# Twelve of 72 weight chunks get their low bits on VectorE alone, in a kernel whose order of work is written out as a string

## The chip, the cores and the metric

The kernel runs on one core of one Trainium2 chip. The metric is the device time of one execution in microseconds. Times before are the median of three runs; one further execution was profiled.

## The reference, cut to what matters

Attention within clusters (16 heads in two batches, 768 positions, head size 64) is followed by two blocks of dense layers over 1,536 tokens:

```python
mask = argmax(q_n . c_n) == argmax(k_n . c_n)        # per head, 16 centroids
attn = softmax(where(mask, q @ k.T / 8, -1e9))
x = attn @ v                                          # to [1536, 512]
h = x @ w_in
g = where(h >= 1, h, where(h <= -1, 0, (h + 1)**2 / 4))
x = g @ w_out                                         # 2048 -> 512
out = ((x @ w1) * (x @ w2)) @ w3 @ w_out2
```

The weights arrive as 64-bit floats and are used as 32-bit ones. The kernel makes each 32-bit pattern from the two 32-bit words of the 64-bit number. That is the work that the change is about.

## The kernel before, in words

**Tiling.** A head pair is a unit: four units for batch 0, four for batch 1. Each unit's attention is cut into 12 tiles of 128 queries by 768 keys, numbered 0 to 95 over the whole kernel; tiles 0 to 47 are batch 0. A tile goes through a score matmul on TensorE (`s`, L859, four instructions into one of four PSUM buffers), a row maximum on VectorE (`smax`, L867), a scale on GpSimd (L872), an exponential on ScalarE (`sexp`, L880), in batch 0 a transpose on TensorE (`spT`, L897) and a copy to SBUF on ScalarE or VectorE (`sT`, L352 or L354), which frees the PSUM buffer. Half a unit ends with a product with v (`pv`, L968) and a transpose of the reciprocal row sums (`ro`, L954). Queries and keys are each split into a rounded part (half-width casts of 64x768: `qh`, `kh`, `k2h`, `q1h`, `qh0`) and a remainder (low parts: `qlo`, `klo`, L357). The clusters come from projections onto the centroids (`am`, L539) and an argmax on VectorE (`ah`, L555 to L573).

**Weight chunks.** 72 chunks of 128x512 numbers are loaded as pairs of 32-bit words and turned into 32-bit floats by the function `chunk`. Each takes four operations: an absolute value with a scale of the high words on ScalarE (`wabs`, L1107), a floor of the low words on ScalarE (`wr`, `low_floor`, L1111), which leaves their top three bits as a number, a shift left by three and an OR on VectorE (`wc 2`, `shift_low`, L1115), and the sign by an AND and an OR on VectorE (`wc 3`, `sign`, L1121). 40 chunks are made in the attention of batch 0. Most of the first 24 are then split into a rounded part (`whi`, a chunk cast, L352 on ScalarE or L354 on VectorE) and a remainder (`wlo`, a chunk subtraction, L357 on GpSimd or VectorE), and multiplied into each other on TensorE (`wp`, L1169), with partial products copied out (`wpe0`) and added later (`wpe`, L1193). Others are stored to DRAM (`wd`, on SP's queue). Batch 0's dense layers run under batch 1's attention, and batch 1's layers after that (L1239, L1492).

**Start.** Eight loads of queries and keys and those of v go out on SP's queue, weight loads on ScalarE's. 40 filler products of the identity with itself (`idle`, L469) stand between TensorE's first steps; tile 6 may not start before all are done.

**Order.** Every step is declared with `add`: its name, the engines that may take it with a planner's costs, its needs and the buffers that it takes and frees. The planner's result is not computed in the kernel. It is written out in `ORDER`, a string of two letters for each of 3,036 steps: the pair, read as a number in base 88 and divided by two, gives the step, and the remainder which of its engines takes it. Each engine works its own steps in this order. Nothing else sets the order of the work.

```python
i, alt = divmod(LETTERS.index(a) * len(LETTERS) + LETTERS.index(b), 2)
```

Of the kernel before, what the change touches and what calls it, by code (L numbers as in the profile page):

```python
# [35 lines left out]

LETTERS = "#$%&()*+,-./0123456789:;<=>?@ABCDEFGHIJKLMNOPQRSTUVWXYZ[]^_`abcdefghijklmnopqrstuvwxyz|~"
ORDER = (
    "###%#*#,#0#.$.$V%X#(%V%[#2$0#4%e%h%c%q$6$8$:$<$>$X$_$a$c$e%b%k$2$4$H%]:m:|%y&,%_%i;0;>$@$B$D%m;L$]$Z$q#B$g$i"
# [4 lines left out]
    ",4,(,*,,,6<6<F<J&9<L<N<8<:<<&E&I<?+m+|,#,.&K,8,:,<<s,%<V,0,2,><g&>%%<@,@,L=*=:<e,B,D+g,N,P,F,R,X,Z,],_<i<k<Z"
    "<n<]<p,e,g<`<a;|<0<2,H,T,a,J<u+i+l,u,w=J<w=X<y<|+o=#%@&@&B<B<Q<R,V,c,y,|=,=<=i=>-(&P=.-#-*+r-,-.-4-6-%-8-:=0"
    "<q=%&c-0-2=@+s=2=4=6=B=D=(%>=y=N-<-@&U-B-D=L=Z=]-L,i,l=P=R=U=V&L-X-Z-]-N-P>0=_,m,o-F->=k>@=a=m=o=d=e=q=s>#-_"
    "=|>P-R-H-u-K-w-y>%>(>4>2>6-e-g=8=F,r-a.(.*.,>D-T-V&_-c&i>a-|>8,s=g=u>+&l&o&e&[=H>-.4.6.8=w>:&W&^&R&b&n>B>F>H"
    ".#-i-m>K&X>L&u..>o.%.0-k.@.B.3.D-o?#>.>=>>%*>e&s.L.N>R>T>V>c&g?4.:.X.<.Z>N>q>s-q.F>X>Z%B.P.R.T.>?(>g>u?%.]?F"
    "._>i.H.J.V>w?*>l>z>]?,?.?0>n>~.a.u.c?V/(/4/*/,&z&|/@-s.w/B/D(&?8?i?@&w>_?2?B?D/.(-($%,/6?6&q?J?H((%D.m.y.|/#"
    "?:?L(.?Z?X?]?<?N/8/:/<?>/%?_?k?m?o?a?Q?q?R/0/2/>%.%0%2.e.g?y%4?s?u/F%F/L/N%H%6/H%J?T?c?e@2@B/J/X%L%8@T@#/P/R"  # L50
    "/T@,?g%:%</Z.i.k?|@4@e0(0*@%.o@(@*/]/_/e/g/V.q?w@.@0/a/c.s@w@6/u/w(*@D0,0.@8@:@=/y@>%N040608@F@H@J@X/|/m@i@V"
    "@g@Z00%P0#0%%R@k@m@]@`@a@N@L@o%T@@@PA.0:020<0?0@0L0N0P0B0D@y@|/i/k/oA2A#A%A)A*0X@q@RA:@c@s@u0u0w0y0FA@0R0T/q"
    "0Z0]APAcA0A40H0J0W0|0_A,A<A>0e0gABADAF(0(2/sA6A8(4(61#0a0c1(1*0iAs1416ATARAVAX0lAZAH1,1.AeAgAiA]AkAKAM1%181:"
    "AwB%0m0o1012AmAo1X1Z1@1L1N1P1B1D1](:Au(=ANA_AaB,1<1R1T(8(AAy(>(BA|(MB#(N1_1FAqB(1H1>B*(D1e1g1J1V(FBJ(H1a1d0r"
    "1i2*(Z(J0s2,2.1u1k1w1y20B.B022(P1|(R24Bi1m1o1rC.BLBO1s2#2%26(TBkBmB2B4B6CL2((V(X282:2<B8B>B@Ck2>BBC12F2H2J2@"
    "2B2DBPBR2LBTBDB;2NB=BV2PBFBIB]B_BaBcBfC2C4C6FLC82T2V2XCNFe2c2eBXCQ2gC:Bg2RBZ2Z2^2_BoBqC<BsB|C#2i2kC?D0BuBxC&"
    "C(2m2a2oC@CBCD3%3(C+(]3*BzCRCTCn3,CoCWCFCH3436383/D>30D3C_CaCcCeC,CX3:3<D#3>2q323B2y3@CK(b3D(d(_(e3P3RCZD@D4"
    "D6D%DLD(3F3HD*3K3L3NCg(h3T3VDZ3XC^3ZD:CjD9CqCsCuCwDB2s3_D<3a3cDN3m3]D]3oCz(iDi3q3e3hDDDG3i3k(tD-E.3sG#(lDHDJ"
    "DPDR2u(nD_4>Da3u3wDk2w2|DTEL(pDn(uC~3#3y4042FP44463|Dc4@4B)(DVE1E2(w4D4GDeDg(q484:4H4JEkD/DYF0ENF>EP(yDoDqDs"
    "4L4N4<4PFiDuDxFND|E#4RFR4#EnFTEoE%E(4TGL4VDz4XFg4ZE4E6E*Fk4]4_E-FmFoE8E:4%4(E@EBF24aG(4*4,Gu4.FVF54c4e4gEEEF"  # L60
    "G%E<E?EI(|)#)%)*G*G,G.F#5:F%F(F*ERETEWEXEKHDE_5<5>F@F6F8FBEaE[E]GPEcEe5@Gy4i4k4m5B5D5FGNGRGT4oEqFYFZEsEuEwF:"
    "4q4s4uF-4w4y4|FqFsEyHmGwG|FHH#F<5H5JHHF/I,EhFJHFEjHJHLGVH%HNFDFFHq5#5,5.5LG05%5(FaFc5*G3E~F]FyF|HoHsHu5N5PHw"
    "F_FuGXGZH)IDI05V5X5R5T5ZH+I.FwI2I4I]G@GBGDGF5]5e5g5i5_5aGHGJ),G4G6).G9)1I65cIa)2G]G_5kHQGa5mHR)4G:G<5s50545u"
    "5oIH52Gc565wGfGgIF5qIJILIN58Iu5y5|6#GiGk6(6*G>GmJDI_HzHTIcGo)66,HV)9GrH~Gs6.60HXHZIe626%64):)<)>H86DH:H<H>H,"
    "H.H0I#6FH26H6R6TI%I8I:JmIyJHIwH@JFI|)AJ#J%)BJJ6JHaHc6V6XHeHgJLI(HCH5JNIgIPIi6Z6]6L6N6PH]6_H_I@K466IRI<I>JqKT"
    "Ik6a6cI*6eJo686g6i)D)FIB6o6q6sHiK86k6mJsJuK66uJ)K:6>IT6w6y6|J*H6IVIXIZJQJSK<K>)NImIoKuKXKVKZHl7#6:6<Jw)H)J)L"
    "K]KyJ,J.Kw6@6BK|L<7%J0J2JTJVJXJZL#7(7*7,IqJ5J6JzJ|Is7.70J^J_LTJ8J:J<J>727476K@KBL%)PK_J@JaJcJeL@JgJiJk7N7PJC"
    "K#K%K)7RKaKcK*KDKF78L>LB7TLV7:LuKH7<KJLD7>7V7XK,K.7@L)L*K0K2KLM4LHLXKeKgLwKNKP7]7_7a7c7eKRLZL]KiLyKm7k7m7gKk"
    "L|MTM#L,L.7oKo7q)T7BLaLcLJ7ZLF7sKr7u7i7wL_KsM8)RM6M%L0)V)X7y7|L47HMVL6L8L2MX8#8%8(Mm8.808284)Z8*L:M:M<LLLeM)"
    "M*MZN48<8>LP8@)_LNLg86Mo)cLS888,8:M]M_Lm7D7F7J7LM>LoM@Ma)^)a)e)gMCLiM,M.8X8Z8B8D8FM0NLN8LqMqMDLl8]8_8g8aMLN6"  # L70
    ")iMdMsLtMu8HNmN:MFMzM~N<M28i8k8mNPMHMeMJ8oMNMiMQMSO,NN)k)m8c8q8sNRN,NA8eNoNqMhNTNCNYNs8J8LNZ8R)o)qNVOLMw)sMk"
    "N.O0NuNw8u8w8y9*9,9.N#N%N)N*NyO.O2O4N~N>90928|OeNDNFOP9496NHNJO8O:Ne9#9%N0O69(NgP,8N8P8T8VONOROTOVN]N_NaOYN2"
    "989:9<9F9H9J9>O#O&O<NdO[9LP0OgP.9T9VNiNk9A9BPD9DO>OiOk9N9POmO(P2OrOsO*O@O]PeOo9R9c9e9gOCODP4OFP69q9sOaOdO_9i"
    "PF9k9mP8OuPHPJPLP;9XPQP#OwP%9u9w9y:%:(:*9|Q#PgOHPN9o:#9[PiOJP(P*PkPSQ%QDPmQ(Q*Q,Po9]9_9aQ.Oy:,:.P@PBP<:4:6Pr"
    "Q0:8:0P]PT:2QN:::=:>PsP>:B:D:F:HPuO|Q3Qa:JP_PbPV:P:RQG:@:TPwQI:L:N:VPX:XPyQ4Q6Q9QQQRP|QJQ<:ZQcQeQkR#PcP[Q;QL"
    "QTQVQ>QAQB:]:gRcR.R_Ra:_:a:cR@QmQp:e:iQZQ^QgR]:kR%R)QiRfS4RJQqQwR*S2RgRjRkR0S)R3S0S9S6QXQ_S]S@SCSEQsQuS;S_SU"
    "SWS=S?RCS$RnRESeSXRvRwSmQySLRqToR,RpRLShROSQR4R:RtTqRzS[R6R8SaSdSOR<R>Q|RFRHSrStS+SjS&SSSuSyS~R~SlTxT#S,T&Tz"
    "TsU%V(SHT~U*SxRPRRU.RTT(T6SGV*SKT,T:U-RVRYRZT0T<SoT.TvT>T@U0U#S.U2U4U6V,V.W:TPTRT2TBTZT]T*T8TFTTTWV0V2V4U(V6"
    "THT_TaTcW<TJU:UBUHU>ULTXV8T4TDUNV<V@VBU<UJW>W@V>TLTNU@UPURUXUZU]TeUcUeTgVEVHXLWBU8WDWFTiTkVLV:UDU_UTTmUmWJUo"
    "UaUgUiWOUqVZUsUkVGWIUuXNXZVTUFUVUwVPW_V_VaVJVRVcWRWmWMUyU|V#VeV%WPVNV]VVWcXPXRVuVwWVWXWZVyXiXwY,VkVnXUX^WaX`"  # L80
    "VgWoWqV|Y.XVXXW%W#X#W(VoXlXmVqVsW*W,XzXeXaX|Z>X&W.WUX(X*XcW^Y5XhY0Y6XoWgWsY9Y:X,Y3Y<YAVXXsViW0ZBZ@YBYDY?WeWu"
    "ZEWwYG[PXqYPY`YTYcZFYHYKWiWyW2W4W7W8ZcZrX8X.X1[_YLZNX:X2ZIX5XuX6Y(Y*ZSZTZKZL[mX<Y#WkW|XBZQYRZeX?X@Ya[S[TXDXF"
    "XIYoYqYs[b[c[oZsYXYeY&XJZgYVZVZX[VYN[(ZZZ_Z][q[ZZk[*[,[/YvYw[|]0[0]2YgYi^BYyY|Z#]#Z%[XYZ[e[iYk[]ZuZ(Z*Z-Y]Ym"
    "ZwZ.]&]8[k]:]<]?]@]D]H]FZ4ZaZ6Z8[w[s^D]4]6Z1Zi[g]C]M]QZyZ2Z|[u^FZ:Z<^J],[y](]K[2[4]N[6^H_T^L_c[8^gZm[#]TZo]X"
    "[:].]]]V]*_V_X[<^u[%]d[>[@[C^N^Q[D]Z^i_q_Z^R_e_h^V^[[F[H^_^a[J]g[L[N__]S]e_s_]`%]i]s_i^w_,^U]k]u]m_a`4]w^c]z"
    "_m]|`B_v_|^#_w^Y`)^%^(`6^+^,_._0`+_o_k_2`u_4`#`8^e^]a*a]`E`F^k^y^o_y^|a_^q_(_@_C]_]o^.^0^m_#_D_%_6]a]q_8^8^:"
    "^s`,^2^4_:`0_*^<_J_G^6ae_Hamagaqai_M_<auak^?_N_P^@aw`x`yaya|_R`H`J_>ap`:`<as`]bR`X`[```>a-a/`@`L`.aabT`N`e`P"
    "`aad`S`hcH`|a#`2`m`pa%a@`T`WaC`db[b]b_bVbYa(a4a6a9aHa0a2aDb(bwa:a=`ib#aGb*bya?`laKb.cLcJbcbgbbcOaTaWb0b&bjd>"
# [1669 lines left out]
```

## Time and profile before

| what | value |
|---|---|
| three runs, median | 719.14 us (718.37 to 720.06) |
| profiled execution, device time | 719.4 us |
| its span | 717.7 us |
| TensorE, VectorE, ScalarE, GpSimd busy | 697.5, 615.3, 467.4, 279.6 us |
| floors of low words on ScalarE (L1111) | 72, of 767 ns on average |
| shift with OR (L1115), sign (L1121) on VectorE | 72 each, of 695 and 726 ns on average |

The span runs from the first to the last instruction of the profiled execution; its device time is 1.7 us longer. Busy times of different engines overlap. The matmuls of TensorE are pipelined and their ends are modelled, so its busy time includes stretches in which it works below its peak; the busy time of its weight loads says how dense a stretch is.

### The profile page before, as it was taken

The page shows a single profiled execution, that of the slowest core. Times are in us where ns is not written, and L with a number is a line of the kernel's source. Part 1 is how long each engine was busy: PE and PEld are TensorE (multiplying, and loading weights), DVE is VectorE, ACT ScalarE, POOL GpSimd, SP SyncE. Part 2 cuts the span into 40 slices and gives each one's busy share as a digit, 9 for nine tenths or more (in the row PEclk, how much of TensorE's full clock was granted, in tenths as well). Part 3 has the DMA queues.
Part 4 walks back from the last instruction along what each step waited for, and adds up shares of the span by engine and source line. Part 5 has one row for each costly group of instructions (what it writes and reads, how often), then busy time and mean ns, then how long its engine had stood idle before and what let it go on. Part 6 is the DMA issues. An engine that isn't in the chain of part 4 may idle for free.

```text
span 717.7 us, 12011 instructions
## 1 busy us (share of the span) xinstructions
PE 697.5 (97%) x4185; PEld 633.1 (88%) x4185; DVE 615.3 (86%) x1087; ACT 467.4 (65%) x873; POOL 279.6 (39%) x351
## 2 busy tenths in 40 slices
...
GB/s 323 85 147 232 296 212 217 293 246 232 229 187 194 227 204 228 193 222 222 232 213 239 227 224 186 136 196 120 45 103 88 46 59 73 59 61 74 87 63 56
DMA packets 122509, 121.58 MB, mean 169 GB/s; under 512 B 80656, under 2 KB 89296, under 8 KB 122448
## 3 DMA queue, kind: packets, MB, share of 16 engines
...
## 4 chain that ended last, share of the span: by engine, by line
PE 80%; ACT 5%; DVE 5%; issue 2%; DMA 1%; ACTq 0%; POOL 0%; SPq 0%; DVEq 0%; POOLq 0%
PE mo L1239 37%; PE sc L1492 9%; PE sc L859 7%; PE mo L1492 6%; PE sc L1239 5%; PE av L976 3%; PE mo L1169 3%; PE av L1239 3%; PE sc L897 2%; PE av L968 2%; PE av L1492 2%; ACT P L880 2%; DVE nm L867 1%; ACT pt L352 1%; DMA wf<-wp 1%
## 5 line engine op out<-in xcount | busy, mean ns | idle before, releaser
L1239 PE MATMUL mo<-X,whl 128*128 128x384 f32 x912 | 169.0, 338 | 0.8 <-DVE Yp L354 0.8
L1239 PEld LDWEIGHTS mo<-X,whl 128*128 128x128 f32 x912 | 158.5, 188 | 3.1 <-DVE Yp L354 1.2
L357 POOL TENSOR_TENSOR whl<-wf,whl 128x512 fp32r<-128x512 f32 x69 | 92.0, 1335 | 128.4 <-DVE whl L354 53.6
L1239 PE MATMUL mo<-G,whl 128*128 128x384 f32 x684 | 126.2, 339 | 0.0
L1239 PEld LDWEIGHTS mo<-G,whl 128*128 128x128 f32 x684 | 120.4, 188 | 0.8 <-ACT phl L352 0.3
L867 DVE TENSOR_REDUCE nm<-sc 128x1 f32<-128x768 f32 x96 | 89.7, 950 | 9.5 <-PE sc L859 6.9
L872 POOL TENSOR_SCALAR nm<-nm 128x1 f32<-128x1 f32 x96 | 30.1, 313 | 132.8 <-DVE nm L867 122.4
L352 ACT ACTIVATE whl<-wf 128x512 fp32r<-128x512 f32 x63 | 39.3, 628 | 36.8 <-PE mo L1239 19.0
L859 PE MATMUL sc<-k,q 128*128 128x512 f32 (+1 forms) x192 | 53.5, 359 | 1.9 <-ACT pt L352 1.2
L1107 ACT ACTIVATE wf<-w 128x512 f32<-128x512 f32 x72 | 48.0, 674 | 11.3 <-POOL whl L357 6.3
L1111 ACT ACTIVATE w<-w,down 128x512 uint32<-128x512 uint32 x72 | 54.6, 767 | 0.2
L880 ACT ACTIVATE P<-sc,nm 128x768 f32<-128x768 f32 x52 | 46.6, 900 | 11.3 <-POOL nm L872 6.6
L1121 DVE SCALAR_TENSOR_TENSOR wf<-w,wf 128x512 uint32<-128x512 uint32 x72 | 51.8, 726 | 1.2
L1115 DVE SCALAR_TENSOR_TENSOR wf<-wf,w 128x512 uint32<-128x512 uint32 x72 | 49.6, 695 | 1.0 <-ACT wf L1107 0.4
L859 PE MATMUL sc<-kq 80*128 80x512 f32 (+1 forms) x192 | 49.4, 339 | 0.0
L880 ACT ACTIVATE sc<-sc,nm 128x768 f32<-128x768 f32 x44 | 38.2, 869 | 15.9 <-POOL nm L872 15.4
L357 DVE TENSOR_TENSOR phl<-sc,phl 128x768 f16<-128x768 f32 x44 | 41.8, 951 | 6.6 <-ACT phl L352 5.9
L897 PEld LDWEIGHTS sc<-ident,P 128*128 128x128 f32 x312 | 35.0, 140 | 10.4 <-ACT P L880 6.8
L897 PE MATMUL sc<-ident,P 128*128 128x128 f32 x312 | 40.7, 275 | 2.4 <-ACT P L880 2.3
L352 ACT ACTIVATE pt<-sc 128x768 f32<-128x768 f32 (+1 forms) x46 | 36.4, 811 | 5.8 <-PE sc L897 4.7
L859 PEld LDWEIGHTS sc<-k,q 128*128 128x128 f32 x192 | 31.5, 189 | 9.0 <-ACT pt L352 3.7
L357 DVE TENSOR_TENSOR whl<-wf,whl 128x512 fp32r<-128x512 f32 x43 | 31.0, 721 | 9.2 <-ACT whl L352 8.7
...
## 6 DMA issues: line engine op xcount, KB each, us to landing
...
```

Of the source, the lines that this page charges most:

```text
L352: nc.scalar.activation(out=out, in_=in_, func=AF.Copy)
L357: (nc.gpsimd if e == "POOL" else nc.vector).tensor_tensor(out=out, in0=a, in1=b, op=ALU.subtract)
L859: nc.tensor.matmul(ps[:, n], q[0:n_rows, q0:q0 + 128], k[0:n_rows, n], start=first, stop=not first)
L867: nc.vector.tensor_reduce(out=nm, in_=T[("sc", b), s], axis=AX.X, op=ALU.max, negate=True)
L880: nc.scalar.activation(out=new(("P", b), s).rearrange("p n s -> p (n s)") if by_pe(s) else T[("sc", b), s], in_=T[("sc", b), s], func=AF.E ...
L897: nc.tensor.transpose(T[("sc", b), s][:, c], p[:, c], ident)
L1107: nc.scalar.activation(out=T["wf", i], in_=T[w64, i].bitcast(F32)[:, :, 1], func=AF.Abs, scale=float(2.0 ** -112))
L1111: nc.scalar.activation(out=lo, in_=lo, func=AF.Identity, scale=float(2.0 ** -29 - 2.0 ** -41), bias=down)
L1115: nc.vector.scalar_tensor_tensor(out=w, in0=w, scalar=3, in1=T[w64, i][:, :, 0], op0=ALU.logical_shift_left, op1=ALU.bitwise_or)
L1121: nc.vector.scalar_tensor_tensor(out=w, in0=T[w64, i][:, :, 1], scalar=0x80000000, in1=w, op0=ALU.bitwise_and, op1=ALU.bitwise_or)
L1239: nc.tensor.matmul(acc, w[:, a, k4 * 128:(k4 + 1) * 128], rhs(c, k4), start=(first and k4 == 0 and n == 0), stop=(last and k4 == 3 and n = ...
L1492: nc.tensor.matmul(ps, lhs(av, a, k), rhs(bv, c, k), start=k == 0 and n == 0, stop=k == 1 and n == 2,)
```

## The change

The odd-numbered ones of the first 24 chunks lose the floor on ScalarE. In its place VectorE shifts the absolute value left by three (`shift`, one tensor and a constant), and the next VectorE operation ORs in the low word shifted right by 29 (`low`). The sign stays. So these 12 chunks take one ScalarE and three VectorE operations, and the other 60 two and two, as before.

```diff
+        def shift(e):
+            w = T["wf", i].bitcast(U32)
+            nc.vector.tensor_scalar(out=w, in0=w, scalar1=3, scalar2=None, op0=ALU.logical_shift_left)
+
+        def low(e):
+            w = T["wf", i].bitcast(U32)
+            nc.vector.scalar_tensor_tensor(
+                out=w, in0=T[w64, i][:, :, 0], scalar=29, in1=w, op0=ALU.logical_shift_right, op1=ALU.bitwise_or
+            )
...
-            add(("wr", i), {"ACT": 0.56}, t - 8.5, low_floor, [("wl", i), "c_const"])
-            add(("wc", i, 2), {"DVE": 0.6}, t - 7.8, shift_low, [("wabs", i), ("wr", i)])
+            if i % 2 and i < 24:
+                add(("wc", i, 1), {"DVE": 0.34}, t - 8.2, shift, [("wabs", i)])
+                add(("wc", i, 2), {"DVE": 0.6}, t - 7.8, low, [("wc", i, 1)])
+            else:
+                add(("wr", i), {"ACT": 0.56}, t - 8.5, low_floor, [("wl", i), "c_const"])
+                add(("wc", i, 2), {"DVE": 0.6}, t - 7.8, shift_low, [("wabs", i), ("wr", i)])
```

The whole of `ORDER` is replaced. Decoded, 367 steps go to another engine, 42 of them ahead of tile 48's maximum, and many change their place by a few positions. These steps of VectorE stand ahead of tile 48's maximum in one order alone:

| only before | only after |
|---|---|
| `k2h` 1.1, 2.1, 3.1; `kh` 2.0; `qh0` 1; `qh` 2.0, 2.1, 3.0, 3.1 | `k2h` 1.0; `kh` 2.1, 4.0; `q1h` 2.0, 3.1 |
| `klo` 0.0, 3.1; `qlo` 4.0 | 12 shifts |
| copies `ri` 0.1, 1.0; `xh` 0.1, 1.0 | copies `ri` 3.1; `xh` 2.1 |
| `whi` 2, 15, 16, 26, 36; `wlo` 6, 36 | `whi` 3, 13, 24; `wlo` 2, 4, 10, 15, 24, 38 |
| `sT` 38 | `sT` 42; `wpe0` of the first product |

Of ScalarE, ahead of tile 48's exponential, the casts and copies of the left column from `k2h` to `xh` (without `klo` and `qlo`), `whi` and `sT` stand only after, those of the right column (without shifts and `wlo`) and the 12 floors only before. TensorE's first steps, with the number of fillers between them (I), are:

```
before: c_T  am k0  am q0  am k1  ah  am q1  I1  ah  I3  vpT  I8  ah  I1  s0  I8  ah  s1 s2 spT0  I5  s3  I8 ...
after:  I1  c_T  I1  am k0  I3  am q0  am k1  ah  am q1  I3  ah  I10  vpT  ah  I1  s0  I7  ah  s1 s2 spT0  I3  s3  I7 ...
```

SP's first loads were k0, q0, k1, q1, k2, k3, q3, q2 and are q0, q1, k0, k1, q2, k3, k2, q3; the second load of v stands ahead of the first store of a chunk and stood behind the third.

## Rows read from the trace of the kernel before

**Rows 1.** The page: the chain that ended last, by engine.
```profile
PE 80%; ACT 5%; DVE 5%; issue 2%; DMA 1%; ACTq 0%; POOL 0%; SPq 0%; DVEq 0%; POOLq 0%
```

**Rows 2.** Table by stages: us; busy PE, PEld, DVE, ACT, POOL; clock; DMA; GB/s.
```profile
0.00:17.70 17.70, 7.15 (x35) 1.69 (x35) 10.99 (x29) 13.41 (x18) 5.31 (x14) 1.00 0.89 321
17.70:24.10 6.40, 6.40 (x40) 6.29 (x41) 5.15 (x9) 4.39 (x8) 1.81 (x1) 0.73 0.21 82
24.10:42.50 18.40, 18.07 (x132) 15.63 (x132) 17.36 (x26) 17.17 (x30) 4.96 (x9) 1.00 0.43 131
42.50:57.90 15.40, 14.56 (x91) 10.66 (x88) 12.89 (x24) 13.66 (x26) 7.26 (x11) 1.00 0.42 127
57.90:110.10 52.20, 51.91 (x311) 38.78 (x310) 49.89 (x79) 49.37 (x86) 21.60 (x27) 1.00 0.76 251
110.10:145.10 35.00, 33.08 (x205) 23.47 (x204) 33.83 (x54) 30.48 (x52) 11.72 (x17) 1.00 0.81 266
145.10:188.70 43.60, 42.24 (x248) 31.53 (x249) 40.11 (x60) 36.29 (x63) 12.01 (x18) 1.00 0.76 232
188.70:250.00 61.30, 61.30 (x374) 56.22 (x371) 55.59 (x91) 44.39 (x84) 21.00 (x32) 1.00 0.94 206
250.00:300.00 50.00, 48.52 (x293) 45.52 (x292) 45.27 (x75) 37.04 (x67) 16.80 (x23) 1.00 0.85 207
500.00:714.00 214.00, 214.00 (x1220) 213.69 (x1219) 169.38 (x355) 93.14 (x208) 103.80 (x119) 1.00 0.22 69
```

**Rows 3.** ScalarE's groups, 17 to 190 us; after the bar: busy us, mean ns.
```profile
L1111 ACT ACTIVATE w<-w,down 128x512 uint32<-128x512 uint32 x40 | 30.3, 772 | 0.0
L352 ACT ACTIVATE wf<-mo 128x512 f32<-128x512 f32 x6 | 3.7, 612 | 0.0
L352 ACT ACTIVATE kq<-kq 64x768 fp32r<-64x768 f32 x4 | 3.4, 843 | 0.5 <-issue 0.4
L352 ACT ACTIVATE whl<-wf 128x512 fp32r<-128x512 f32 x5 | 3.2, 641 | 0.3 <-DVE wf L1121 0.3
```

**Rows 4.** VectorE's groups, 24 to 189 us.
```profile
L1115 DVE SCALAR_TENSOR_TENSOR wf<-wf,w 128x512 uint32<-128x512 uint32 x40 | 27.5, 697 | 0.7 <-ACT wf L1107 0.4
L354 DVE CAST kq<-kq 64x768 fp32r<-64x768 f32 x11 | 6.0, 548 | 0.2
L354 DVE CAST whl<-wf 128x512 fp32r<-128x512 f32 x11 | 4.7, 423 | 0.1
L357 DVE TENSOR_TENSOR q<-kq,kq 64x768 fp32r<-64x768 f32 x3 | 2.8, 950 | 0.1
L357 DVE TENSOR_TENSOR whl<-wf,whl 128x512 fp32r<-128x512 f32 x4 | 2.7, 687 | 0.1
L354 DVE COPY wf<-mo 128x512 f32<-128x512 f32 x2 | 1.4, 692 | 0.9 <-PE mo L1169 0.9
```

**Rows 5.** Timeline of the start: start us, duration us, instruction [idle before it].
```profile
7.78 1.87 PE L539 MATMUL sc<-kq,cT 128*32 128x384 f32 x8 [1.67 <-DVE cT L450]
10.91 0.56 DVE L568 TENSOR_TENSOR phl<-P,amx 128x384 bf16<-128x384 f32 x1
16.82 0.85 PE L539 MATMUL sc<-kq,cT 128*32 128x384 f32 x8 [2.52 <-DMA kq<-in_qT_dram]
18.69 1.81 POOL L357 TENSOR_TENSOR q<-kq,kq 64x768 fp32r<-64x768 f32 x1 [5.55 <-ACT kq L352]
19.93 0.99 DVE L568 TENSOR_TENSOR phl<-P,amx 128x384 bf16<-128x384 f32 x1
23.94 1.95 PE L469 MATMUL av<-ident 128*128 128x128 f32 x16
```

**Rows 6.** VectorE's waits, 24 to 189 us: total us, times, longest us.
```profile
DVE nm L867 <- PE sc L859: 3.5, 8, 1.3
```

**Rows 7.** The chain that ended last, 20 to 120 us, by line.
```profile
by line: PE mo L1169 11.2%; PE sc L859 10.9%; PE sc L897 9.7%; PE av L968 8.0%; ACT P L880 8.0%; issue 6.3%; ACT pt L352 4.4%; DVE nm L867 3.7%; ACT wf L1107 2.4%; ACTq L1101 1.9%; ACT w L1111 1.7%; ACTq L728 1.4%; ACT kq L352 1.1%; ACT k L
```

**Rows 8.** GpSimd's groups, 8 to 190 us.
```profile
L357 POOL TENSOR_TENSOR whl<-wf,whl 128x512 fp32r<-128x512 f32 x12 | 16.6, 1382 | 37.6 <-DVE whl L354 23.5 <-ACT whl L352 9.5 <-issue 4.6
```

More of the change, by code (lines that the diff above doesn't have):

```diff
@@ L44 @@
[L44 to L88, printed above, removed]
@@ new lines @@
+    "+B+D+:+.&6*i<T*k<6+0+<*o;s+L+2+N+P+X+Z+]<(&/&&<*;u<,<.;x;y&9*r;Z;j*s&4&:&D+F+R+T+H&<%(+>+_+u+J+V+a+c<c<X+w<F"
+    "+y<s<8+|,4,(,6,8,*,:,,<H<J,.<:%>%@<<;k<L<N&F&K+e&I+m,#<?<@,%=*,0,<,2,><V&N,@,L,B,D<e,N,F,X,Z+g,P,R=:<Z<g<i<]"
+    "<k<`<n;|<0<2<b,],_,e<p,T,H,J+i+k<u<w=J,a,u&@&B,w,V,c,y,|<y<|=#&P+o<B<Q<R=,+q=X=<=>-(-*-,-.=.,g-4-#-6=@+s-%=B"
+    "=D-8-:<q=0&c&M=2=5=6=L=N-0-2&T=]=i=%=(-@-<-B-D->=Z-L-X-Z-F=y>0=P=R=T=_=a=W&S&Z=c=e-N,m,i,k,o&k=k-]-P-H-u-w-y"
+    "-K=m=o>@&b=q=s-R-_-e-g&W,q&_=8=F=H.(.*=|>#>2>4,s>%>6>P-a-T-V-c>a>(-|=g=u&i&^>8>:>+&e=w.,.4.6.8>D>o>B.#..?#.%"
@@ new lines @@
+    "&n>F>->H>K>L&X-m-i-k-o.0%B&u&g>e.@.B.D.3.:>.>=>>>R>T?4>c>q.L.N>V-q&o.X.<.Z&s>X?(>N>Z>s>g.F>u.P.R>i.T.H.>?F?%"
+    ".]._?*>w>l.a>z?,>n.u?/.J.V?V&q>].c?@/(%*>_/4>~?1&y&|($/@-s/B/D.w.y?2&w(,?B?D?i?6?8?Z?H(%%,/*/6()?:.e%D?J.|?L"
+    "?<?>?X?]?N?_?a/,/.?y/8/:.m?m/#/%/</0?k?o?q/2/>%.%0%2%4@2?P?R%F/F?s/L%H/N%6/P?c%J@B/H?|/J(.@,?T?u/X%8?e@T@6/R"
+    "/T@#%L.g%:%<?g/Z/].i.k.o@%0(0*0,@4@(@*@F/_.q.s/V?w@.@0/a/c/e/u/w@8%N/y@e@w(*@D@H@J@:@=@>/g/|0.@V/m04%P0608%R"
+    "@X@Z@]@`@a@N@LA.%T0#00@i@g@k@@@P@R0%0:@m020<0>0L0@0N@y@|A#0P0B0D@qA@A%A)A*0X/i/k@oA2AP0RA:0u0w0y@c@s@u0F0H0T"
```

59 lines of the change are left out of this document (47 added, 12 removed).

## The prediction

> **What bounds the kernel now.** I read the page first, for the chain that ended last, then the table by stages, then the groups and the waits of the stage that the change touches. TensorE holds 80% of the chain [rows 1]. The table by stages shows two regimes. From 188.7 us on (tile 48's maximum) TensorE is idle for next to nothing: 0.0 of the first 61.3 us, 1.5 of the next 50.0, 0.0 of the 214 before the end [rows 2]. There nothing but TensorE's own work counts. Before 188.7 us, in the attention of batch 0, TensorE is less full than its busy time says: its weight loads, which fill 213.7 of 214 us at the end, fill 38.8 of 52.2 us here, and the busy time of pipelined matmuls covers the difference [rows 2]. In this stage VectorE is busy for 49.9 of 52.2 us and ScalarE for 49.4 (57.9 to 110.1 us); from 110.1 to 145.1 us VectorE has 33.8 of 35.0 and ScalarE only 30.5 [rows 2]. So three engines share the bound up to 110 us, and VectorE is the tighter of the two small ones after it. The kernel moves by what happens before tile 48, as long as TensorE stays full afterwards.
>
> **What is removed and added.** The first 24 chunks are complete before tile 30's maximum in both orders, so every saving and every cost falls into this stage. Removed: 12 floors on ScalarE at 0.77 us [rows 3], 9.2 us. Added: 12 shifts on VectorE. The second operation of the new three keeps the form of the present one, two tensors from SBUF, one of them strided by two words; at 0.70 us [rows 4] I count no change for it. The shift has no row. Its bounds are the cast of a 128x512 chunk, 0.42 us, and the two-tensor operations of that size, 0.69 to 0.70 us [rows 4]. It has one tensor input and lies wholly in SBUF, as the cast does, so I take 0.42: 5.0 us in all, 8.3 at the other bound; no row offers it for less.
>
> **What is moved.** I decoded both order strings against the list of steps: 367 of 3,036 take another engine, 42 of them ahead of tile 48's maximum. Up to the last product of batch 0's attention TensorE's 147 steps other than fillers are the same set, and all 40 early chunks are complete before tile 48's maximum in both orders. Up to there VectorE gives away nine half-width casts and four 384-wide copies (counted alike, 0.55), three low parts (0.95), five chunk casts (0.42), two chunk subtractions (0.69) and a tile copy: 13.5 us and the tile copy. It takes the 12 shifts, five half-width casts, two 384-wide copies, three chunk casts, six chunk subtractions, a partial product's copy (0.69) and another tile copy: 15.0 us and the tile copy [rows 4]. **VectorE's sum is +1.5 us.** ScalarE loses the 9.2 us and the partial product's copy (0.61); it gains four half-width casts net (0.84), two 384-wide copies (some 0.5) and two chunk casts (0.64) [rows 3], 5.6 us: **-4.2 us.** GpSimd, busy for 21.6 of 52.2 us [rows 2], has room for its share.
>
> Summed in the same way up to earlier tiles, VectorE stands at -0.6 at tile 8's maximum, +1.2 at tile 12's and again at tile 36's; ScalarE at -1.8, -2.8 and -4.8 at the exponentials of these tiles.
>
> **The start.** The new order puts five of the 40 filler products ahead of the first transpose and the first projections, where TensorE waits anyway (for centroids, 1.7 us [rows 5]), and leaves 35 behind the last projection. That one starts at 16.82 us after 2.5 us of waiting for the last of eight loads [rows 5], which is the eighth in the new order too. From 17.7 us TensorE is busy without a gap to 24.1 and for 18.1 of the next 18.4 us [rows 2]. At full clock eight fillers pass in 1.95 us [rows 5], 0.24 each with what stands between them; five fewer are worth 1.1 to 1.2 us. VectorE can follow: its work to tile 8 falls by 0.6 us, because one low part goes to GpSimd, where its like takes 1.8 us [rows 5], in a gap ahead of tile 0; and 1.0 of these 18.4 us is idle time [rows 2]. I take -1.0. Bounds: 0.0, if tile 0 is held back by the fillers in front of it (14 after the last projection, 13 before), while the clock granted from 17.7 to 24.1 us averages 0.73 [rows 2]; and -1.6, VectorE's work and all its idle time.
>
> On SP's queue the first query loads pass the key loads, so that the fourth load, no longer the third, releases the first projection, and the second load of v passes the first three stores of chunks, which wait for VectorE. Neither ends a wait of TensorE now: the first projection waits for VectorE's centroids [rows 5], and the last of the eight loads keeps its place. I cost them at nothing. Without that cover a place in the queue costs a 384 KB load, about 1.2 us at the 321 GB/s of these first microseconds [rows 2].
>
> **The middle.** From tile 8's maximum (42.5 us) to tile 48's (188.7) VectorE has 2.1 us more to do (+1.5 after -0.6). It is idle for 9.5 of those 146.2 us [rows 2]. The largest wait, 3.5 us, ends with a score matmul [rows 6], and those wait for buffers that ScalarE empties; ScalarE has 2.4 us less to do in this stretch. Bounds: no wait shrinks, +2.1; half of the idle time goes, -2.6. I take **0.0**, the value at which the new work just fills old waits: where VectorE has least idle time, from 57.9 to 145.1 us, its sum does not change (+1.2 at both ends), and the 1.8 us that it gains between tiles 8 and 12 fall where it stands idle for 2.5 of 15.4 us [rows 2].
>
> **The rest.** Behind tile 48 the other 325 steps change engine. TensorE's idle time there is 1.5 us [rows 2], so that much is to be gained; as much may be lost. I take 0.0. The tail, a ScalarE copy and a store behind the last product, keeps its engine.
>
> **Sum.** -1.0 + 0.0 + 0.0 = -1.0 us. The profiled execution took 719.4 us (its span of 717.7 and 1.7 around it), which makes 718.4; it lies 0.3 above the median of 719.14, so on the median's scale I predict **718.1 us**.
>
> **The rivals.** *ScalarE sets the pace, and its relief counts in full* (25%). For it: between 20 and 120 us the chain passes through ScalarE's exponentials and copies, 8.0 and 4.4%, more than through VectorE's maxima, 3.7% [rows 7]. Against it: VectorE's 96% of the densest stage. Half of VectorE's idle time goes, -2.6 - 1.0 = -3.6 us: 715.5.
>
> *VectorE sets the pace* (17%), on the other side. No wait shrinks between tiles 8 and 48, the 2.1 us stand, and the start gives back 0.6: +1.5 us, 720.6. It decides if the new work stands in front of maxima that TensorE waits for, so that less than about a quarter of the 9.5 us of idle time can be filled.
>
> *The shift costs what a two-tensor operation costs* (6%). Another 3.3 us on VectorE, half to all of it beyond what idle time takes: -1.0 + 1.6 to 3.3, 719.7 to 721.4 us.
>
> *Shifts wait for GpSimd* (2%). One argmax operation took 0.99 us beside a GpSimd subtraction, and 0.56 without one [rows 5]. GpSimd is busy for 41% of the densest stage [rows 2]; were all of that its chunk subtraction of 1.38 us [rows 8], a shift would wait 0.41 x 0.69 = 0.28 us on average, 12 shifts 3.4: 721.5 us at most. Against it: the chunk casts of this stage average 0.42 us [rows 4], so they hardly wait.
>
> The Trainium skill (SBUF — State Buffer, Who interferes with whom) states that a VectorE operation in a two-port mode and a GpSimd operation lock each other out, and that ScalarE waits for nobody; by it, moving work off ScalarE buys a risk. By that rule the one argmax operation agrees and the casts of this stage show next to nothing of it.
>
> *The searched order places work worse behind tile 48* (8%): +1.5, 719.6 us or a little more, the start's gain gone.
>
> **Chances.** The forecast's own case has 42%, with a range of 717.0 to 719.6. A measurement of this kernel can tell a change of about 0.2%, 1.4 us. Below 717.7 us lie a third of the forecast's case and the first rival: 39%. Above 720.6 lie two thirds of the second rival, half of the third, the fourth and parts of the last and of the forecast's tail: 22%. Within: 39%. With two in ten left out the range is 715.4 to 721.0 us.
>
> **What would show it.** Right: 60 floors on ScalarE in place of 72, and 12 shifts near 0.42 us; VectorE busier by some 1.5 us ahead of tile 48's maximum, ScalarE less busy by some 4; tile 8's maximum near 41.5 us and tile 48's near 187.7; TensorE without idle time behind it. Wrong: shifts of 0.7 us; tile 48's maximum beyond 189 us; more than 2 us of idle time of TensorE behind it, or matmuls that it stretches over; or VectorE's idle time ahead of tile 48 down by 4 us, which would be the first rival.

## The result, and the profile after

Six executions of the changed kernel on the chip of the first comparison took 723.9 to 733.0 us, median 726.62, against 719.11 us before: a ratio of 1.0105, 95% interval 1.008 to 1.013. On another chip it was 727.23 against 719.75, 1.0099 [1.0078, 1.012]. The change costs 1%, some 7.5 us; the forecast was 718.1 us, with 721.0 as the upper end. The profiled execution took 729.26 us with a span of 727.5, 9.8 more than before.

The page after, the chain that ended last, by engine [rows 1]:

```profile
PE 72%; DVE 13%; DMA 8%; issue 3%; ACT 2%; POOL 1%; SPq 1%; ACTq 0%; DVEq 0%; POOLq 0%
```

TensorE's part falls from 80 to 72%; VectorE's grows from 5 to 13 and that of transfers from 1 to 8. ScalarE, whose floors were removed, falls from 5 to 2, and nothing is won by it.

The table by stages after, cut at the maxima of tiles 0, 8, 12, 28, 36 and 48 as before [rows 2] (us; busy PE, PEld, DVE, ACT, POOL; granted clock; DMA; GB/s):

```profile
22.90:41.80 18.90, 16.54 (x115) 13.89 (x115) 16.67 (x29) 16.56 (x29) 3.96 (x8) 1.00 0.34 101
41.80:57.50 15.70, 15.27 (x97) 11.46 (x93) 15.04 (x25) 14.91 (x27) 7.16 (x11) 1.00 0.48 165
57.50:115.80 58.30, 53.82 (x310) 39.76 (x310) 50.26 (x83) 47.85 (x86) 17.72 (x26) 0.97 0.68 223
115.80:151.00 35.20, 33.51 (x205) 23.33 (x204) 33.49 (x55) 31.82 (x54) 10.20 (x14) 1.00 0.70 241
151.00:194.50 43.50, 42.73 (x251) 32.26 (x252) 40.03 (x62) 34.32 (x61) 14.92 (x21) 1.00 0.76 244
500.00:714.00 214.00, 213.01 (x1209) 211.59 (x1208) 180.71 (x381) 91.49 (x204) 105.39 (x120) 1.00 0.23 71
```

Three things are to be seen. Tile 0's maximum comes 1.2 us sooner (22.9 against 24.1), but behind it TensorE is idle for 2.4 of 18.9 us, where it was idle for 0.3 of 18.4, and tile 8's is only 0.7 sooner. The stage from tile 12 to tile 28 takes 58.3 instead of 52.2 us, with a mean clock of 0.97: here nearly the whole loss of the first half arises. And TensorE, which was never idle in the 214 us before the end, now is for 1.0 us.

The operations themselves are as forecast. Groups of VectorE (24 to 195 us) and of ScalarE (17 to 196 us) after [rows 3, 4]:

```profile
L1115 DVE SCALAR_TENSOR_TENSOR wf<-wf,w 128x512 uint32<-128x512 uint32 x28 | 19.1, 682 | 0.2
L1125 DVE SCALAR_TENSOR_TENSOR wf<-w,wf 128x512 uint32<-128x512 uint32 x12 | 8.5, 711 | 0.1
L1121 DVE TENSOR_SCALAR wf<-wf 128x512 uint32<-128x512 uint32 x11 | 4.6, 420 | 3.0 <-ACT wf L1107 3.0
L1111 ACT ACTIVATE w<-w,down 128x512 uint32<-128x512 uint32 x28 | 21.1, 764 | 0.1
```

The shift takes 0.42 us, and the join with the low bits 0.71. From tile 8's maximum to tile 48's VectorE has 138.8 us of work instead of 136.7, the forecast's +2.1 to a tenth. But that stage lasts 152.7 us instead of 146.2, and VectorE's idle time in it grew from 9.5 to 13.9 us.

**The stall at 96 us.** The timeline of ScalarE, VectorE and TensorE there (start us, duration us, instruction, [idle before it]), and the table for the gap and for what follows it:

```profile
94.01 0.49 ACT L352 ACTIVATE X<-av 128x384 fp32r<-128x384 f32 x1
...
96.53 0.95 DVE L357 TENSOR_TENSOR q<-kq,kq 64x768 fp32r<-64x768 f32 x1
...
97.51 0.96 DVE L867 TENSOR_REDUCE nm<-sc 128x1 f32<-128x768 f32 x1
97.57 1.28 ACTq L728 DMA_DIRECT2D kq<-mask  x2
...
98.98 0.60 ACT L352 ACTIVATE wf<-mo 128x512 f32<-128x512 f32 x1 [4.48 <-DVE nm L867]
...
99.63 1.65 PE L1183 MATMUL mo<-X,whl 128*128 128x512 f32 x3 [3.77 <-ACT wf L352]
```

```profile
95.80:99.70 3.90, 0.12 (x2) 0.07 (x1) 2.57 (x5) 0.72 (x2) 1.48 (x2) 0.97 0.29 86
99.60:104.20 4.60, 4.57 (x14) 3.64 (x15) 2.74 (x6) 4.00 (x7) 0.00 (x0) 0.64 0.91 287
```

ScalarE's next step after 94.5 us is the issue of two mask copies into the kq tile of pair 2's second head. VectorE still has to read that tile for q's low part, and in the searched order it comes to it only at 96.53, behind the new operations on chunk 17 and others. The issues start at 97.57, 0.09 us after the low part has ended, take 1.28 us, and only then does ScalarE empty the PSUM bank that TensorE wants. The view names VectorE's maximum as ScalarE's releaser, because that is the last instruction near it; the start of the ACTq row shows the true one. TensorE stands for 3.8 us, and for the 4.6 us behind it its granted clock averages 0.64, so the twelve matmuls of this product take 4.5 us, against 2.9 for the like product before it. In the old order the copies are issued ahead of that low part (at 95.9 us, the low part at 101.6), and there is no such wait. The two orders are not quite the same work here. By the row ranges in the kernel the copies write rows 64 to 79 of that tile, and the low part reads rows 64 to 127: the old order reads these sixteen rows after they have been overwritten, the searched order before. What that does to the output is not part of this record.

**The later wait.** A second gap of 3.5 us stands at 377.6 us in this execution, and small ones lie behind 452 us. TensorE's waits from 452 us to the end, which in the kernel before has no row at all:

```profile
PE mo L1506 <- DVE G L357: 0.8, 1, 0.8
PE mo L1253 <- DVE tmp L354: 0.6, 1, 0.6
PE av L1506 <- DVE X L357: 0.2, 1, 0.2
PE mo L1253 <- DVE whl L357: 0.2, 1, 0.2
```

### The profile page after: what moved, and what is told of

It is laid out like the page before. It is cut to its first block, busy times and chain, and to the rows that moved or that the text cites. A ratio compares the mean times of both kernels' runs of the same rounds, so it can differ in the third digit from the quotient of the medians.

```text
span 727.5 us, 12018 instructions
## 1 busy us (share of the span) xinstructions
PE 700.0 (96%) x4185; PEld 633.7 (87%) x4185; DVE 611.2 (84%) x1093; ACT 466.6 (64%) x870; POOL 278.6 (38%) x348
## 4 chain that ended last, share of the span: by engine, by line
PE 72%; DVE 13%; DMA 8%; issue 3%; ACT 2%; POOL 1%; SPq 1%; ACTq 0%; DVEq 0%; POOLq 0%
PE mo L1253 31%; PE sc L859 7%; PE sc L1506 7%; PE sc L1253 6%; PE mo L1506 5%; PE mo L1183 4%; PE av L976 3%; PE av L968 3%; DMA pt<-phl 3%; PE sc L897 3%; DVE nm L867 2%; PE av L1506 2%; DMA wd<-wf 2%; DMA kq<-in_kT_dram 1%; DVE wf L1131 1%
## 5 line engine op out<-in xcount | busy, mean ns | idle before, releaser
L1253 PE MATMUL mo<-G,whl 128*128 128x384 f32 x708 | 131.7, 340 | 0.8 <-DVE tmp L354 0.6
L357 POOL TENSOR_TENSOR whl<-wf,whl 128x512 fp32r<-128x512 f32 x62 | 83.4, 1346 | 118.2 <-ACT whl L352 49.6
L1253 PEld LDWEIGHTS mo<-G,whl 128*128 128x128 f32 x708 | 124.3, 188 | 2.9 <-DVE tmp L354 0.9
L352 ACT ACTIVATE whl<-wf 128x512 fp32r<-128x512 f32 x72 | 45.0, 627 | 55.6 <-PE mo L1253 23.1
L1131 DVE SCALAR_TENSOR_TENSOR wf<-w,wf 128x512 uint32<-128x512 uint32 x72 | 50.1, 703 | 0.9
L1111 ACT ACTIVATE w<-w,down 128x512 uint32<-128x512 uint32 x60 | 45.3, 763 | 2.7 <-DVE wf L1131 1.1
L1115 DVE SCALAR_TENSOR_TENSOR wf<-wf,w 128x512 uint32<-128x512 uint32 x60 | 43.4, 722 | 3.5 <-ACT wf L1107 2.0
L357 POOL TENSOR_TENSOR wh<-ws,wh 128x256 fp32r<-128x256 f32 x40 | 32.6, 825 | 27.8 <-ACT wh L352 15.5
```

The source lines that it names most:

```text
L352: nc.scalar.activation(out=out, in_=in_, func=AF.Copy)
L357: (nc.gpsimd if e == "POOL" else nc.vector).tensor_tensor(out=out, in0=a, in1=b, op=ALU.subtract)
L1111: nc.scalar.activation(out=lo, in_=lo, func=AF.Identity, scale=float(2.0 ** -29 - 2.0 ** -41), bias=down)
L1115: nc.vector.scalar_tensor_tensor(out=w, in0=w, scalar=3, in1=T[w64, i][:, :, 0], op0=ALU.logical_shift_left, op1=ALU.bitwise_or)
L1131: nc.vector.scalar_tensor_tensor(out=w, in0=T[w64, i][:, :, 1], scalar=0x80000000, in1=w, op0=ALU.bitwise_and, op1=ALU.bitwise_or)
L1253: nc.tensor.matmul(acc, w[:, a, k4 * 128:(k4 + 1) * 128], rhs(c, k4), start=(first and k4 == 0 and n == 0), stop=(last and k4 == 3 and n = ...
```

## Experiments

Medians are those of the timed executions; ratios are to the kernel before on the same chip, with 95% intervals. "Old" and "searched" order are those of before and after.

### Order or operations?

```diff
 first: the searched order
-k2(2,1)              # the two mask copies, behind xh(1,0)
 wpe0(4), wabs(18), wr(18), wabs(19)
+k2(2,1)
```

> The changed kernel with one step put six places later: the two mask copies of unit 2's second head (k2 2.1, on ScalarE's queue) stand behind the absolute value of chunk 19, not ahead of a partial product's copy. Theory A (ScalarE's queue stands 4.5 us at these copies, which wait for the low part that reads the rows they overwrite; TensorE then waits 3.8 us for the one PSUM buffer of the products): TensorE's gap at 96 to 100 us is gone, and 4 to 5.5 us with it, 720 to 723 us. Theory B (VectorE has too much to do because of the shifts): no gain, 725 to 728. Theory C (the new order is worse in many small places): a gain of 0 to 2.

```diff
 second: the kernel after, each step in its place of before
-ORDER = searched
+ORDER = old, with each shift just ahead of its join
```

> The chunk change alone, in the order of the kernel before: the 12 shifts stand directly ahead of the operation that follows them, nothing else moves, and ScalarE lacks 12 floors. Theory A: the chunk change does no harm of its own; -1 to +2 us against the kernel before, 718 to 721. Theory B: VectorE's 5 us of shifts stand on the path, 722 to 725. Theory C: 718 to 721.

```diff
 third: the kernel before, floors and all
-ORDER = old
+ORDER = searched, each odd chunk's floor where its shift stands
```

> The new order with the 12 floors kept on ScalarE in the shifts' places: no chunk change, only the order. Theory A: the wait of the mask copies stays, since what they wait for stands in the same place; 724 to 730 us, some of it from the floors that ScalarE has again. Theory B: back to 719 to 721. Theory C: 724 to 730, without one place that holds most of it.

The fourth is the kernel after unchanged, on the chip of the other three.

> The changed kernel once more, for a second profile, since its six runs spread over 9 us and those of the kernel before over 1.7. Theory A: the gap of TensorE at 96 to 100 us is there again with some 3.8 us; the second gap of the first profile (3.5 us at 377 us, behind a transposing transfer that took 12.1 us to land) need not be, and then this profile is 3 to 4 us shorter. Theories B and C: gaps elsewhere, the sum alike.

| kernel | median us | ratio |
|---|---|---|
| mask copies later | 726.06 | 1.0091 [1.0074, 1.0108] |
| change, old order | 722.92 | 1.0047 [1.003, 1.0064] |
| floors, searched order | 733.09 | 1.0189 [1.0169, 1.0208] |
| after again | 727.23 | 1.0099 [1.0078, 1.012] |

By the medians, the twelve chunks' new operations in the old order cost 3.2 us; the searched order with floors in the shifts' places costs 13.3. Together they cost 7.5. So the order is made for the operations that it has, and 4.3 of the 7.5 come only with it. Moving the copies back did not free ScalarE. TensorE's and ScalarE's longest waits at 90 to 110 us there:

```profile
PE sc L788 <- ACT pt L351: 2.4, 1, 2.4
```

```profile
ACT pt L351 <- DVE X L356: 3.1, 1, 3.1
```

ScalarE reached the same copies a few steps later, still before VectorE had done the low part (it ended at 97.92 us, the copies went out at 97.95); the wait moved from one PSUM buffer to another.

### Which engine sets the pace?

```diff
 low part first: the searched order
+qlo(2,1)
 wc(17,1)             # chunk 17's shift
 ...
 rr(1,1)
-qlo(2,1)
```

> Theory (the stall ahead of TensorE's matmuls for wp chunk 5 comes from ScalarE standing at the mask copies of pair 2, second head, whose source rows VectorE's low part of q still reads; moving the copies back only moved the stall): with VectorE making that low part some 3 us sooner, ahead of chunk 17's shift, the copies need not wait, TensorE's 3.8 us gap at 96 to 100 us and the slow clock behind it are gone, and about 5.5 us come back: near 721.5 us against 727 for the kernel after. Rival (the reordered work behind 90 us is short of something else, and the wait moves again as it did in the first try): another gap of 2 us or more opens before 110 us, and the time stays near 726 us.

```diff
 floors gone: before, old order, odd i < 24
-add(("wr", i), {"ACT": 0.56}, t - 8.5, low_floor, ...)
-    out=w, in0=w, scalar=3, in1=T[w64, i][:, :, 0], op0=..., op1=ALU.bitwise_or
+    out=w, in0=w, scalar=3, in1=w, op0=..., op1=ALU.bitwise_and
```

> The order of before with ScalarE's twelve floors taken out and nothing put in their place (the low bits of these twelve chunks are left out). Theory (VectorE sets the pace ahead of tile 48, ScalarE's relief is worth nothing there): within 0.7 us of the kernel before, 719.4. Rival (ScalarE sets the pace, and the relief of 9.2 us is worth something that the shifts then eat): 3 us or more below before, 716.5 or less.

```diff
 more shifts: before, in shift_low
+if i % 2 and i < 24:
+    nc.vector.tensor_scalar(out=w, in0=w, scalar1=0, scalar2=None, op0=ALU.logical_shift_left)
```

> The order of before with all sixty floors kept and twelve more VectorE shifts (by 0 bits) in the places where the change puts its own. Theory (the 5.0 us more of VectorE's work are what costs, whatever ScalarE does): 2.5 to 3.5 us above before, about 722.4. Rival (the loss in the old order is not VectorE's time but the chunks' new waits): within 1 us of before, under 720.4.

```diff
 casts to ScalarE: the change in the old order
-VectorE: whi 1, 6, 8, 10, 11, 15, 16, 18, 20; qh(2,0), kh(2,0)
+ScalarE: the same, in the same places
```

> The change in the old order, and eleven casts of the first 120 us (nine high parts of weight chunks, two of q and k) given from VectorE to ScalarE: about 5.0 us less on VectorE, 7.2 us more on ScalarE, so both stand about where they stood before. Theory (VectorE's load sets the loss of 3 us): the loss goes, 719 to 720.3 us. Rival (the loss sits in the order of the steps, not in VectorE's load): 722.5 us or more. If ScalarE is as close to being the bound as VectorE, the time also stays above 721.5, with ScalarE's waits shrinking and VectorE's growing in the stretch from 40 to 120 us.

```diff
 less on VectorE: before, and the change in the old order
-VectorE: wlo 1, 6, 11, 18, 22, 23
+GpSimd: the same, in the same places
```

> The kernel before, all sixty floors, in its own order, with the low parts of six weight chunks (1, 6, 11, 18, 22, 23; some 4.0 us in all) given from VectorE to GpSimd, which is busy 45 of the 120 us from 20 to 140. Theory (VectorE's load sets the pace ahead of tile 48 in the kernel before too): 2 to 3.5 us faster than before, 716.2 to 717.7 us. Rival (the order of before is held by each wait in turn, so taking work off VectorE pays no more than taking it off ScalarE did): within 1 us of 719.7, or above it where GpSimd's small score biases now stand behind a low part of 1.3 us.

> The change in the old order, and the same six low parts given to GpSimd: VectorE stands 1 us above its load of before, ScalarE 9.2 us below. Theory (VectorE's load is the loss of 3.2 us): 719 to 720.5 us. Rival (not its load but the place of the three operations): 722 us or more.

```diff
 joins gone: before, old order, odd i < 24
-add(("wc", i, 2), {"DVE": 0.6}, t - 7.8, shift_low, [("wabs", i), ("wr", i)])
```

> The kernel before in its own order, all floors kept, with VectorE's join of shift and low bits left out for the twelve odd chunks (twelve operations of about 0.68 us, 8.2 us in all; their weights lack the shift and the low bits). It is the mirror of the run without floors. Theory (VectorE's work sets the pace ahead of tile 48): 3 to 6 us faster than before, 713.5 to 716.5 us. Rival (this order was searched until no engine's relief pays; each engine has to hand over at given places, and only what is added counts): within 1 us of before, 719.4.

```diff
 first six: the change in the old order
-if i % 2 and i < 24:
+if i % 2 and i < 12:
```

> The change in the old order for chunks 1 to 11 alone, six of the twelve: 2.5 us more on VectorE, 4.6 us less on ScalarE. Theory (VectorE's work counts wherever it stands ahead of tile 48): half the loss of the whole change in the old order, about 721 us. Rival (it counts only where chunks 13 to 23 are made, behind 80 us, since with all twelve tile 18 still came at its old time): within 0.8 us of before.

| kernel, old order | VectorE, ScalarE | median us | ratio |
|---|---|---|---|
| floors gone | 0, -9.2 us | 718.97 | 0.9999 [0.9983, 1.0014] |
| joins gone | -8.2, 0 | 719.22 | 0.999 [0.998, 1.000] |
| more shifts | +5.0, 0 | 723.64 | 1.0068 [1.0042, 1.0094] |
| change, first six | +2.5, -4.6 | 721.00 | 1.0022 [1.0004, 1.0039] |
| six low parts to GpSimd | -4.0, 0 | 722.66 | 1.004 [1.0027, 1.0053] |
| change, six low parts to GpSimd | +1.0, -9.2 | 725.95 | 1.0088 [1.0073, 1.0104] |
| change, eleven casts to ScalarE | 0, -2.0 | 739.59 | 1.0278 [1.0257, 1.0298] |

The column in the middle is what the edit adds or takes, by the mean durations of the operations. The first kernel leaves out the low bits of the twelve odd chunks, the second the whole operation that shifts and joins them; both are only there to be timed. The first two rows decide. Neither engine's relief alone buys anything that a measurement can tell, 9.2 us on the one and 8.2 on the other. The theory that VectorE sets the pace forecast 3 to 6 us for the joins, and falls. The table from 20 to 140 us shows why: in the kernel before, floors gone, joins gone, and the change in the old order, in this sequence:

```profile
20.00:140.00 120.00, 116.62 (x734) 88.63 (x733) 112.44 (x178) 109.29 (x187) 45.16 (x59) 0.99 0.65 212
```

```profile
20.00:140.00 120.00, 117.08 (x738) 88.80 (x738) 113.35 (x180) 103.49 (x178) 44.76 (x59) 1.00 0.64 215
```

```profile
20.00:140.00 120.00, 115.84 (x726) 87.76 (x726) 104.18 (x165) 108.02 (x186) 43.59 (x58) 1.00 0.62 210
```

```profile
20.00:140.00 120.00, 114.91 (x719) 86.09 (x717) 115.01 (x188) 101.97 (x174) 42.99 (x58) 1.00 0.62 206
```

TensorE is busy for 116.6 of 120 us (9.7 of them with fillers), and its matmuls are no longer here than where it never idles: in the kernel before, the second part of a score averages 396 ns (`kq`, 80x512) from 24 to 140 us and from 189 to 250 us, and the product with v 490 and 486 ns. So its busy time here is its own work, and fillers aside only the other 3.4 us could be gained in this window. A run that relieves both engines at once was not made; it could have won no more than that. But VectorE, with 7.6 us idle, stands right behind TensorE: 5.0 us more, and TensorE's idle time grows to 5.1 in this window. Additions count where relief does not, with or without the floors (more shifts against the change in the old order, whose intervals overlap), and less for six chunks than for twelve: 1.3 us, with an interval of 0.3 to 2.8, which is too wide to call it half.

Moving VectorE's work to GpSimd lost 3 us, and to ScalarE far more, since each cast or low part stands there in front of something small that TensorE waits for. With the eleven casts on ScalarE, TensorE's longest waits from 20 to 140 us are

```profile
PE sc L896 <- ACT pt L351: 6.4, 2, 5.3
PE sc L896 <- ACT P L879: 5.6, 5, 3.3
```

and ScalarE's own longest one is for a weight chunk's sign that VectorE has not done, behind which the exponentials queue:

```profile
ACT whl L351 <- DVE wf L1130: 8.4, 3, 4.1
```

On GpSimd two low parts in a row held a score bias back (idle before the exponential: 2.29 us), and VectorE's casts beside its subtractions took longer. The kernel before with six low parts on GpSimd, timeline:

```profile
120.67 2.86 POOL L356 TENSOR_TENSOR wo<-wf,wo 128x512 fp32r<-128x512 f32 x2
...
123.62 0.19 POOL L871 TENSOR_SCALAR nm<-nm 128x1 f32<-128x1 f32 x1
123.84 0.90 ACT L879 ACTIVATE P<-sc,nm 128x768 f32<-128x768 f32 x1 [2.29 <-POOL nm L871]
123.89 1.83 POOL L356 TENSOR_TENSOR q<-kq,kq 64x768 fp32r<-64x768 f32 x1
...
124.72 1.41 DVE L353 CAST kq<-kq 64x768 fp32r<-64x768 f32 x1
```

### Where the searched order loses

The low part made sooner removed the stall: TensorE's 3.8 us gap is gone (the longest wait from 90 to 110 us is 1.1 us), and tile 48's maximum comes at 191.0 us, not 194.5. Yet the median was 727.01, ratio 1.0101 [1.0068, 1.0134], with executions from 722.4 to 730.6. So hybrids of the two orders were run:

```diff
-ORDER = searched, low part first
+ORDER = searched, low part first, up to s(54), s(72) or s(90); from there old
 mirror: old (change in it) up to s(54); from there searched
 stall kept: searched as in after up to s(90); from there old
```

> The kernel after with its stall at 96 us mended (VectorE's low part of pair 2 ahead of chunk 17's shift), and every step from tile 54's scores on in the order of before. Theory (the searched order loses twice: at 96 us, and 3 to 5 us more in small gaps behind 340 us): what is left is the loss at tile 48, 2.3 us, so 721.5 to 722.5 us. Rival (the late gaps are chance of single executions, as the 12.1 us transfer was, and the order behind tile 54 costs nothing): no better than the mended kernel with the new order all through, 725 to 727 us.

> The mirror of it: the change in the order of before up to tile 54's scores, and from there on the searched order. Theory (the later part of the searched order costs 3 to 5 us by itself): 726 to 728 us, against 722.9 for the change in the old order all through. Rival (it costs nothing by itself): 722 to 724 us.

> The searched order with the mended stall, back to the order of before from tile 72's scores on, some 315 us into the span. If the loss of the later part sits between tiles 54 and 72 (the transfer wait at 205 us in the mended run): about 725 us or more. If it sits behind tile 72: 722 to 723.5 us, as when going back at tile 54.

> The same, back to the order of before from tile 90's scores on, some 427 us into the span. If the loss sits in the tiles' stage, where the transposing transfers of SyncE come late: 725 to 727 us. If it sits behind the tiles, in the output stages from 460 us on: 722 to 724 us.

> The searched order with its stall at 96 us left in, back to the order of before from tile 90's scores on. If the stall is worth its own length where nothing takes it up later (3.5 us at tile 48 in the profiles): 724 to 726 us, against 721.3 with the stall mended. If the later part of the searched order is the whole loss and the stall is made good before tile 90: 721 to 722.5 us.

> The mended kernel with the searched order all through, once more. If stall and later part add up, 3 to 4 us below the kernel after, some 723 to 724 us, and the first median of 727.0 was scatter. If 726 to 728 us again: what the mended stall gives is lost again in the later part of this order.

| kernel | median us | ratio |
|---|---|---|
| mended, old from tile 54 | 722.91 | 1.0057 [1.0035, 1.008] |
| mended, old from tile 72 | 721.91 | 1.0032 [1.0017, 1.0047] |
| mended, old from tile 90 | 721.30 | 1.0039 [1.0016, 1.0061] |
| stall kept, old from tile 90 | 724.96 | 1.0074 [1.0045, 1.0102] |
| mended, searched all through, again | 724.88 | 1.0073 [1.0043, 1.0102] |
| old up to tile 54, then searched | 723.22 | 1.0065 [1.004, 1.009] |

The medians look as if two losses add up: with both mended 721.3; with the stall alone 725.0; with the later part alone 724.9 (726.0 over both tries, 17 executions); with both 727.2. But the executions scatter, these kernels ran on different chips, and the intervals of the rows with and without the stall overlap: the times alone do not prove its price. The profiled executions, cut at tile 48's maximum, keep the two losses apart:

| kernel (profiled executions) | tile 48's maximum, us | from there to the end of the span, us |
|---|---|---|
| before | 188.8 | 528.9 |
| change, old order | 191.7 | 529.4 |
| after; after again | 194.5; 194.4 | 533.0; 530.5 |
| stall kept, old from tile 90 | 195.2 | 527.5 |
| mended, searched all through, two tries | 191.0; 191.5 | 534.7; 536.2 |
| mended, old from tile 54; 72; 90 | 191.0; 189.9; 190.6 | 529.7; 528.4; 528.8 |
| old up to tile 54, then searched | 190.7 | 533.2 |
| mask copies later | 193.1 | 529.8 |
| floors, searched order | 200.7 | 530.3 |

The three with the stall reach tile 48 at 194.4 to 195.2 us, the five in which it is mended at 189.9 to 191.5: it costs 3 to 5 us there. The seven that end in the searched order need 529.8 to 536.2 us from there on, those that end in the old order 527.5 to 529.7: this second loss goes from next to nothing to some 7 us, by the execution. Going back at tile 90 is as good as going back at tile 54, so it lies mainly behind tile 90. The second try's profiled execution shows its mechanism at its largest: timeline, and the table for the gap and the stretch behind it:

```profile
449.37 12.27 SPq L926 DMA_TRANSPOSE pt<-phl  x3
...
458.40 0.81 ACT L351 ACTIVATE phl<-sc 128x768 f16<-128x768 f32 x1 [3.80 <-DMA pt<-phl]
...
459.24 0.96 DVE L356 TENSOR_TENSOR phl<-sc,phl 128x768 f16<-128x768 f32 x1 [3.18 <-ACT phl L351]
...
461.99 0.55 DVE L353 COPY tmp<-mo 128x384 f32<-128x384 f32 x1
```

```profile
459.40:462.60 3.20, 0.01 (x1) 0.01 (x1) 3.20 (x5) 1.12 (x3) 1.37 (x1) 0.87 0.57 116
462.60:467.00 4.40, 4.40 (x14) 4.40 (x15) 1.00 (x2) 0.00 (x0) 0.00 (x0) 0.50 0.67 198
```

A cast of probabilities needs a buffer that a transposing transfer still reads. ScalarE waits for the transfer, VectorE's subtraction waits for ScalarE, and behind that subtraction on VectorE stands the copy that would empty TensorE's PSUM bank. The next cast wants the buffer about as soon as in the kernel before, 5.3 us after the subtraction that fills it, against 5.4. The transfers land later. In the kernel before, where no engine waits for them at this place (440 to 466 us), and in this execution (445 to 465 us), count and median us from issue to landing:

```profile
pt<-phl SPq DMA_TRANSPOSE x4, 3.7
```

```profile
pt<-phl SPq DMA_TRANSPOSE x3, 8.9
```

In the kernel after (450 to 466 us) it is 7.3 us. What differs beside them are loads of partial products from ScalarE's queue: here three of 256 KB are issued from 449.2 to 450.5 us, as the first of these transfers starts; in the kernel before one is, at 450.4 us, among the four. That these loads hold the transfers up is read from the coincidence; no run moved them alone. ScalarE's waits for these transfers from 200 to 470 us, in the kernel before, after, and going back at tile 90:

```profile
ACT phl L352 <- DMA pt<-phl: 1.0, 1, 1.0
```

```profile
ACT phl L352 <- DMA pt<-phl: 8.5, 3, 5.9
```

```profile
ACT phl L351 <- DMA pt<-phl: 4.3, 3, 3.2
```

After's gap at 377 us begins with the same wait: there a transfer landed after 12.1 us. How long it lasts follows the transfers of the single execution, which fits the wide scatter. The mirror run fits by its profiled execution (725.6 us, with 9.2 us of these waits), but not by its median, which lies only 0.3 above that of the change in the old order, within executions from 721.1 to 729.8. So the size of the later loss, 0.3 to 4.7 us by the pair of medians compared, stays open; its place is shown by the hybrids, its mechanism is read from the traces. No version was faster than the kernel before.

## Why the prediction was wrong

**The bound** was misread first. The forecast took TensorE's thin weight loads ahead of tile 48 as a sign that TensorE is less full there, and that three engines share the pace. Its own rows have as many loads per us there as at the end (310 in 52.2 us, 1,219 in 214), only shorter ones, and the matmuls are as short as where TensorE never idles. TensorE is nearly full, and the runs without floors and without joins show that neither ScalarE nor VectorE alone could give anything back.

**"The middle", 0.0** is the step that failed: from tile 8's maximum to tile 48's the kernel after takes 6.5 us longer, where the bounds were -2.6 and +2.1. It failed on two counts. That new work "just fills old waits" is refuted by the change in the old order: from tile 8 to tile 48 VectorE has 140.5 us of work, 3.8 more than before, its idle time stays at 9.0 us against 9.5, and the stage takes 3.3 us longer. Read so, the waits are hand-overs at given places, not slack that other work can move into. The bound "no wait shrinks" was right for the operations; the value in the middle was not. The second count had no term at all: moving steps put q's low part behind new VectorE work and ahead of the mask copies that overwrite part of its source, and ScalarE's whole queue stood behind those copies. By the profiled executions this wait is worth 3 to 5 us at tile 48. The medians with and without it differ by 1 to 4 us, which their intervals do not set apart from zero. The forecast counted the moved steps by their durations and asked of two queues, SP's and GpSimd's, what is moved past what; it didn't ask it of ScalarE's own queue of DMA issues.

**The start, -1.0:** tile 0's maximum came 1.2 us sooner, but it did so too in the old order with the old fillers (22.9 us), so the fillers are not shown to be the cause. TensorE then waited 2.4 us behind tile 0, and by tile 18 nothing was left.

**The rest, 0.0:** "as much may be lost" was meant as 1.5 us. In the two profiled executions of the kernel after, the stretch behind tile 48's maximum is 1.6 and 4.1 us longer than before. The rival with the worse order behind tile 48 had the right sign, 8% and too small a price; the wait for transposing transfers was in nobody's sum.

**What held:** the shift at 0.42 us; 60 floors; VectorE's work +2.1 us. ScalarE fell by 0.9 us from tile 8 to 48, where 2.4 was forecast. *ScalarE sets the pace* is refuted by the run without floors. *VectorE sets the pace* came nearest for the operations: no wait shrank, and in the old order the middle grew by 3.3 us, where it said 2.1. That its price (720.6) lies near the mended kernel that goes back at tile 90 (721.3) is partly luck, and relief of VectorE pays nothing, as the run without joins shows. *The shift costs as a two-tensor operation* is refuted. *Shifts wait for GpSimd* shows nowhere in the changed kernel: 420 ns on average. The Trainium skill's rule that a VectorE operation in a two-port mode and a GpSimd operation lock each other out (SBUF — State Buffer, Who interferes with whom) is borne out among the casts where GpSimd got more work: with six more low parts there, VectorE's eleven casts of 64x768 from 20 to 140 us average 774 ns, against 548 before.
